# Block products for the output projection of tiles 5 and 6, wider transposes, and a new order of pieces, in an attention and cosine feed-forward kernel

## The chip, the cores and the metric

The kernel runs on one core of a Trainium2 chip. The core's engines work side by side, each through its own queue in order: TensorE (PE, matmuls; its weight loads are shown as PEld), VectorE (DVE), ScalarE (ACT), GpSimd (POOL), and SyncE (SP), which issues the transfers. The metric is the device time of one execution in microseconds; lower is better.

## The reference, cut to what matters

```python
# attention in chunks of 64 tokens: batch 8, heads 8, 576 tokens, head size 64
scores = scale * np.matmul(q_c, k_c.transpose(0, 1, 2, 4, 3))
scores = scores - np.max(scores, axis=-1, keepdims=True)
attn = np.exp(scores)
attn = attn / (np.sum(attn, axis=-1, keepdims=True) + 1e-09)
x = np.matmul(attn, v_c)            # laid out as 4608 tokens x 512
# feed-forward
h = x @ w_in                        # 512 -> 2048
g = h * np.cos(h)
out = g @ w_out                     # 2048 -> 512
```

## The kernel before

**Tiles and products.** The 4608 tokens are worked on in nine tiles of 512, t = 0 to 8. A product of float32 matrices is made of three fast matmuls: each operand is split into a high part (a cast, `g_hi`, L338 on DVE or L340 on ACT) and a low part (a subtraction, `g_lo`, L344), and high x high, high x low and low x high are added up in PSUM. Each output block is so 128 rows by 512 columns (128x512) or by 256 (128x256).

**Hidden product x @ w_in.** Tiles 0 and 1 are multiplied plainly, tile 2 with two-by-two blocks inside the tile (`two_pairs`). Tiles (3,4), (5,6) and (7,8) go as pairs, u = 1, 2, 3. For a pair the hidden columns are made in eight steps k, two column blocks at a time, with seven block products where eight would be plain: A11, S3, S2, A12, S1, A22, S4. Their sums are taken through PSUM: ACT copies one accumulator into the bank in which the next goes on (`copy_b`, `copy_c`, `copy_d`, L967), and DVE makes two additions (`add_c`, `add_b`, L970). The chain h -> g = h cos h is `whole` (ACT, L973), `turn` (DVE, L976), `sine` (ACT, L980) and `times` (DVE, L983). The bank that S4 fills is read by that chain, and the next step's `copy_b` can write its own bank only when a bank of this kind is free.

**Output projection g @ w_out.** Before, for u = 1 and 2 (`wide_pair`), it is plain: 128x512 matmuls into `acc`, 192 for each tile; the second tile's g is stored to DRAM (`gathered`) and read back (`second_tile`). For u = 3 (`block_pair` with `block_products`) it also goes by seven block products, P1 to P7, on 128x256 matmuls: DVE and POOL make sums of 128x256 blocks of g, the sums are stored to DRAM (`sums`) and loaded back with differences of w_out (`diffs`) for the later products.

**Attention.** Its pieces for later tiles are laid between the products: scores (64x64 matmuls), maximum, exponentials, sums, quotient, 32x32 transposes on DVE (`turned`, L636 and L640), and the weighted values. For (t, g) in `CHUNKED` the exponential of each 64-column chunk is its own ACT instruction, which also gives the sum; otherwise DVE subtracts the maximum, ACT takes the exponential of a wide piece, and DVE sums it. `wide_x` splits the attention's result of a pair of tiles into the fourteen parts that the seven hidden products need.

**Order.** The program is a list of pieces, `work`. `in_order(work, RANK, ELSEWHERE)` sorts it by the hand-kept table `RANK`, and `ELSEWHERE` lists pieces that run on their other engine (ACT for DVE, POOL for DVE). So each engine's queue follows that one order:

```python
place = sorted(range(len(work)), key=lambda i: (rank[i], i)) if rank else range(len(work))
return [(i, work[i][8][0] if i in elsewhere else work[i][0]) for i in place]
```

Of the kernel before, what the change touches and what calls it, by code (L numbers as in the profile page):

```python
# [44 lines left out]
CHUNKED = ((3, 1), (4, 1))  # L45
# [2453 lines left out]
```

## Time and profile before

| | |
|---|---|
| time, median of 3 runs | 776.09 us (774.72 to 777.68) |
| span of the profiled execution on the engines | 773.5 us |
| times of the three runs beside that span | 777.68, 774.72 and 776.09 us |
| PE busy | 762.5 us (99%), 6100 instructions |
| DVE busy | 644.4 us (83%), 1112 instructions |
| ACT busy | 444.8 us (58%), 818 instructions |
| POOL busy | 267.1 us (35%), 245 instructions |
| transfers | 177.22 MB, 66.2% of the 16 DMA engines' span on the main queue |

The profile is of one execution. The span is what the engines took from their first instruction to their last; the time of a run is the device's own and holds the span and some 2.6 us around it (776.09 less 773.5). Busy is the sum of an engine's instructions; a matmul's shown duration overlaps the next one's, so the rate of matmuls is read from a long unbroken row of them: its length over their number.

### The profile page before, as it was taken

The numbers are of one execution on the slowest core, as the hardware profiler recorded it, in microseconds if no ns is written. First come the engines' busy times: TensorE is split into PE (matmuls) and PEld (weight loads), VectorE is DVE, ScalarE is ACT, GpSimd is POOL, SyncE is SP. The second block draws the span as 40 slices with busy tenths as digits, with TensorE's granted clock in tenths as the row PEclk, the third lists the DMA queues.
The fourth block names the chain that finished last, engine by engine and source line by source line (L and its number), as shares of the span: only waits on it lengthen the run. The fifth ranks groups of instructions, "written<-read, shape, count | busy, mean of one in ns | idle before, by whom it ended". The sixth has DMA issues, their size and how long they took to land.

```text
span 773.5 us, 16085 instructions
## 1 busy us (share of the span) xinstructions
PE 762.5 (99%) x6100; PEld 676.3 (87%) x6100; DVE 644.4 (83%) x1112; ACT 444.8 (58%) x818; POOL 267.1 (35%) x245
## 2 busy tenths in 40 slices
PE   7999999999999999999999999999999999999997
PEld 6888888888999988888888888888888888989997
DVE  5998989989899889897898868785998577798874
ACT  5999876456874456554553435546554355557651
POOL 3422133776542444246222321200202315265231
PEclk9999999999999999999999999999999999999999
DMA  9995600579979753777974545587535567988983
GB/s 341 401 410 197 205 2 1 190 263 382 320 255 310 243 165 108 226 259 243 326 265 140 174 135 188 181 290 242 179 104 180 158 208 229 294 300 284 361 305 103
DMA packets 95757, 177.22 MB, mean 229 GB/s; under 512 B 9152, under 2 KB 39872, under 8 KB 95680
## 3 DMA queue, kind: packets, MB, share of 16 engines
q1 hardware_dynamic: 95104, 175.15, 66.2%
q8 instruction: 48, 0.79, 0.4%
q10 hardware_dynamic: 576, 1.05, 0.4%
q14 instruction: 29, 0.24, 0.1%
HBM read 127.93 MB, written 48.23 MB: 228 GB/s over the span
## 4 chain that ended last, share of the span: by engine, by line
PE 84%; DVE 8%; DMA 4%; ACT 2%; issue 1%; SPq 0%; DVEq 0%; ACTq 0%
PE acc L323 39%; PE h L323 33%; PE a L323 12%; DMA w_in<-sums 2%; DMA sums<-qt 1%; DMA combo<-w_in 1%; DVE w_in L970 1%; DMA kt<-in_kT_dram 1%; DVE z L595 0%; DVE w_in L344 0%; DVE pts L640 0%; DVE w_in L937 0%; DVE g L724 0%; DVE m L546 0%; DVE g L726 0%
## 5 line engine op out<-in xcount | busy, mean ns | idle before, releaser
L323 PE MATMUL acc<-w_out,g_hi 128*128 128x512 f32 (+1 forms) x976 | 278.1, 369 | 0.0
L323 PE MATMUL h<-x,w_in 128*128 128x512 f32 (+1 forms) x960 | 226.4, 364 | 0.1
L323 PEld LDWEIGHTS acc<-w_out,g_hi 128*128 128x128 f32 x976 | 178.5, 189 | 22.9
L323 PEld LDWEIGHTS h<-x,w_in 128*128 128x128 f32 x960 | 171.1, 189 | 22.7 <-ACT g_hi L340 0.4
L323 PE MATMUL acc<-w_out,g_lo 128*128 128x512 f32 (+1 forms) x488 | 179.2, 367 | 0.0
L344 POOL TENSOR_TENSOR g_lo<-g,g_hi 128x512 fp32r<-128x512 f32 x30 | 41.4, 1380 | 194.3 <-ACT g_hi L340 70.9
L323 PEld LDWEIGHTS acc<-w_out,g_lo 128*128 128x128 f32 x488 | 92.4, 189 | 11.8 <-DVE g_lo L344 0.2
L323 PE MATMUL h<-w_in,w_in 128*128 128x512 f32 (+1 forms) x384 | 98.3, 354 | 0.8 <-DVE w_in L970 0.7
L323 PEld LDWEIGHTS h<-w_in,w_in 128*128 128x128 f32 x384 | 65.6, 190 | 9.7 <-DVE w_in L970 2.0
L980 ACT ACTIVATE w_in<-w_in 128x512 f32<-128x512 f32 x64 | 39.3, 628 | 17.8 <-DVE w_in L976 17.7
L344 DVE TENSOR_TENSOR g_lo<-g,g_hi 128x512 fp32r<-128x512 f32 x59 | 44.1, 747 | 4.0 <-ACT g_hi L340 2.2
L340 ACT CAST g_hi<-g 128x512 fp32r<-128x512 f32 x48 | 29.7, 618 | 27.8 <-PE acc L323 14.5
L323 PE MATMUL a<-w_in,w_in 128*128 128x512 f32 (+1 forms) x204 | 42.5, 348 | 0.0
L323 PE MATMUL a<-x,w_in 128*128 128x512 f32 (+1 forms) x192 | 41.2, 353 | 0.0
L344 POOL TENSOR_TENSOR g_lo<-w_in,g_hi 128x512 fp32r<-128x512 f32 x12 | 18.9, 1577 | 64.3 <-ACT g_hi L340 42.6
L323 PEld LDWEIGHTS a<-w_in,w_in 128*128 128x128 f32 x204 | 34.5, 190 | 4.0
L323 PEld LDWEIGHTS a<-x,w_in 128*128 128x128 f32 x192 | 33.2, 190 | 4.1
L967 ACT COPY a<-h 128x512 f32<-128x512 f32 x28 | 16.0, 571 | 32.3 <-PE h L323 32.1
L723 ACT ACTIVATE g<-h 128x512 int32<-128x512 f32 x32 | 19.3, 602 | 26.1 <-PE h L323 26.0
L973 ACT ACTIVATE w_in<-h 128x512 int32<-128x512 f32 x32 | 19.1, 597 | 26.3 <-PE h L323 24.7
L976 DVE SCALAR_TENSOR_TENSOR w_in<-w_in,h 128x512 f32<-128x512 int32 x32 | 21.9, 685 | 12.6 <-ACT w_in L973 11.8
L344 DVE TENSOR_TENSOR g_lo<-w_in,g_hi 128x512 fp32r<-128x512 f32 x34 | 28.8, 855 | 3.8 <-ACT g_hi L340 3.2
(294 smaller groups left out, 1509.6 us busy)
## 6 DMA issues: line engine op xcount, KB each, us to landing
w_in<-combo SPq DMA_DIRECT2D x84, 512.0 KB, 4.8
combo<-w_in SPq DMA_DIRECT2D x56, 256.0 KB, 4.5
w_in<-combo SPq DMA_DIRECT2D x56, 256.0 KB, 5.3
qt<-in_qT_dram SPq DMA_DIRECT2D x36, 256.0 KB, 5.6
w_in<-in_w_in_dram SPq DMA_DIRECT2D x16, 512.0 KB, 9.7
kt<-in_kT_dram SPq DMA_DIRECT2D x32, 256.0 KB, 5.6
w_out<-in_w_out_dram SPq DMA_DIRECT2D x16, 512.0 KB, 9.9
gathered<-w_in SPq DMA_DIRECT2D x32, 256.0 KB, 3.7
```

What stands on the lines that cost most here:

```text
L323: kept(nc.tensor.matmul(*args, **kw))
L340: kept(nc.scalar.copy(out=out, in_=in_))
L344: kept(eng.tensor_tensor(out, a, b, op=op))
L723: lambda: kept(nc.scalar.activation(n, h, AF.Identity, bias=0.25, scale=0.5 / math.pi)),
L967: kept(nc.scalar.copy(out=out, in_=in_))
L970: kept(nc.vector.tensor_tensor(out, a, b, op=ALU.add))
L973: kept(nc.scalar.activation(g.bitcast(I32), h, AF.Identity, bias=0.25, scale=0.5 / math.pi))
L976: kept(nc.vector.scalar_tensor_tensor(g, g.bitcast(I32), -2.0 * math.pi, h, op0=ALU.mult, op1=ALU.add))
L980: kept(nc.scalar.activation(g, g, AF.Sin, bias=0.5 * math.pi))
```

## The change

Six things are changed.

- `BLOCKED` grows from the pair u = 3 to u = 2 and 3, so tiles 5 and 6 go through `block_pair` and `block_products` too.
- `CHUNKED` grows by (5,1), (6,1), (7,1), (8,1).
- `turned` takes a group of two head pairs at once: six transposes of twice the width take the place of twelve. Their room is one fixed `pair_room`.
- In each pair, S1 is issued ahead of A22 (in `block_pair` it was already), and `add_b` ahead of `add_c`, so S4 waits for the first addition and no longer for both.
- `times` may run on POOL where its input lies in SBUF.
- `RANK` and `ELSEWHERE` are new.

Counted over the whole program, before -> after: PE 128x512 matmuls 2736 -> 2352, 128x256 matmuls 1008 -> 1680, 64x64 groups of attention 29 -> 33 (in the first 30 us 8 -> 6). DVE transposes 168 of 256 columns -> 84 of 512; DVE casts of 512 columns -8, copies +4, reductions of 512 columns -8, subtractions of a maximum -8, additions of 128x256 48 -> 110, additions and products of 128x512 453 -> 431. ACT casts of 512 columns 163 -> 211, chunk exponentials of 64 columns on 128 partitions 40 -> 104, exponentials of 1024 columns 10 -> 2. POOL additions of 128x512 125 -> 193, of 128x256 114 -> 118. SP: 48 more stores of `sums` and 16 fewer of `gathered`, with the loads that go with them.

```diff
-CHUNKED = ((3, 1), (4, 1))
+CHUNKED = ((3, 1), (4, 1), (5, 1), (6, 1), (7, 1), (8, 1))
...
 RANK = (
-    35, 32, 39, 45, 48, 40, 16, 50, 63, 68, 66, 54, 72, 80, 85, 79, 75, 83, 89, 91, 92, 82, 97, 100, 104, 101, 88,
...
-    def turned(t, hp):
-
-        if t > 2 and hp >= 2:
-
-            pts = weights_of(t, 0)[:, hp % 2].rearrange("p c k -> p (c k)")
+    def turned(t, g):
+
+        if t > 2 and g:
+
+            pts = weights_of(t, 0).rearrange("p a c k -> p (a c k)")
         elif t == FAST + 2:
-            pts = half_room(U_ROOM, hp)
+            pts = w_in_room(U_ROOM, F32)[:, PAD : PAD + 2 * TOK]
         else:
-            pts = att.tile([P, TOK], F32, name="pts")
-        probs[t, hp] = pts
-        src = weights_of(t, hp // 2)[:, hp % 2].rearrange("p c (x k) -> p c x k", k=BL)
+            pts = pair_room.rearrange("p a n -> p (a n)")
+        for j in range(2):
+            probs[t, 2 * g + j] = pts[:, j * TOK : (j + 1) * TOK]
+        src = weights_of(t, g).rearrange("p a c (x k) -> p (a c) x k", k=BL)
...
-    def times(g, h):
-        kept(nc.vector.tensor_tensor(g, h, g, op=ALU.mult))
+    def times(g, h, by=DVE):
+        two_by(by, g, h, g, ALU.mult)
...
-    BLOCKED = range(UNITS - 1, UNITS)
+    BLOCKED = range(UNITS - 2, UNITS)
...
-        a22 = prod(A22, "c", cc)
-        s1 = prod(S1, "b", cc)
-        addc = piece(DVE, 0.69, add_c, a22, cd, *of("h2"))
-        addb = piece(DVE, 0.69, lambda: add(v["h3"], v["b"], v["ds"]), s1, cd, addc)
+        addb = piece(DVE, 0.69, add_b, s1, cd, *of("h2"))
+        addc = piece(DVE, 0.69, add_c, a22, cd, addb)
         s4 = prod(S4, "b", addb)
```

**The joint before tiles 7 and 8.** This is PE's queue where the weighted values of tile 8 are done and the hidden product of tiles 7 and 8 begins. Before, `acc` are the plain projections of tile 6 (102 matmuls of 128x512 in a row up to the first `h`), `x_0` and `x_1` are the high and low part for A11, and `x2` means two such in a row:

```order
L323 MATMUL acc_6925<-w_out_1327,g_hi 128x512 x2
L323 MATMUL acc_6925<-w_out_1327,g_lo 128x512
L323 MATMUL acc_6917<-w_out_1392,g_hi 128x512 x2
L323 MATMUL acc_6917<-w_out_1392,g_lo 128x512
L323 MATMUL h<-x_0_6943,w_in_6765 128x512
L323 MATMUL h<-x_1_7091,w_in_6765 128x512
L323 MATMUL h<-x_0_6943,w_in_6765 128x512 x2
```

The same place after the change, where the projections are block products of tiles 5 and 6:

```order
L336 MATMUL acc_7805<-w_in_7361,g_hi 128x256 x2
L336 MATMUL acc_7805<-w_in_7361,g_lo 128x256
L336 MATMUL acc_7805<-w_in_7361,g_hi 128x256 x2
L336 MATMUL acc_7805<-w_in_7361,g_lo 128x256
L336 MATMUL h<-x_0_7386,w_in_7166 128x512
L336 MATMUL h<-x_1_7398,w_in_7166 128x512
L336 MATMUL h<-x_0_7386,w_in_7166 128x512 x2
L336 MATMUL h<-x_1_7398,w_in_7166 128x512
L336 MATMUL h<-x_0_7386,w_in_7166 128x512
L336 MATMUL a_7873<-w_in_7783,w_in_7166 128x512
```

Ahead of A11 now stand 84 matmuls of 128x256 in a row in place of the 102 of 128x512, and behind A11 comes S3 (`a_7873`) at once.

**Between two steps of tiles 7 and 8.** PE's queue from the end of the first step to the A11 of the second. Before, projections (`acc`) stand between the last matmul of S4 (the first row) and A11 (`h<-x_0`); behind these rows come S3 and, after three more projections, S2:

```order
L323 MATMUL h<-w_in_7072,w_in_7104 128x512
L323 MATMUL acc_6939<-w_out_1554,g_hi 128x512 x2
L323 MATMUL acc_6939<-w_out_1554,g_lo 128x512
L323 MATMUL acc_6925<-w_out_1459,g_hi 128x512 x2
L323 MATMUL acc_6925<-w_out_1459,g_lo 128x512
L323 MATMUL acc_6917<-w_out_1554,g_hi 128x512 x2
L323 MATMUL acc_6917<-w_out_1554,g_lo 128x512
L323 MATMUL h<-x_0_6943,w_in_7104 128x512
L323 MATMUL h<-x_1_7091,w_in_7104 128x512
L323 MATMUL h<-x_0_6943,w_in_7104 128x512 x2
L323 MATMUL h<-x_1_7091,w_in_7104 128x512
L323 MATMUL h<-x_0_6943,w_in_7104 128x512
```

After, the rows begin with the last of S4 (`w_in_7886`); A11, S3 and S2 (`w_in_7764`) follow it:

```order
L336 MATMUL h<-w_in_7886,w_in_7525 128x512
L336 MATMUL h<-x_0_7386,w_in_7525 128x512
L336 MATMUL h<-x_1_7398,w_in_7525 128x512
L336 MATMUL h<-x_0_7386,w_in_7525 128x512 x2
L336 MATMUL h<-x_1_7398,w_in_7525 128x512
L336 MATMUL h<-x_0_7386,w_in_7525 128x512
L336 MATMUL a_7979<-w_in_7783,w_in_7925 128x512
L336 MATMUL a_7979<-w_in_7803,w_in_7925 128x512
L336 MATMUL a_7979<-w_in_7783,w_in_7925 128x512 x2
L336 MATMUL a_7979<-w_in_7803,w_in_7925 128x512
L336 MATMUL a_7979<-w_in_7783,w_in_7925 128x512
L336 MATMUL h<-w_in_7764,w_in_7925 128x512
```

The projections between are gone from this place; nothing but A11's six and S3's six matmuls stands between S4 and S2 here.

**Transposes and additions on DVE.** DVE's queue in a step of tiles 5 and 6, where an attention tile's weights are transposed (L640 and L636) between the two additions of the step (L970). Before, `a_6255` is the bank of `add_c`, `h` that of `add_b`:

```order
L640 STREAM_TRANSPOSE e_5749<-e_5786 32x8x32
L636 STREAM_TRANSPOSE e_5749<-e_5786 128x8x32
L976 SCALAR_TENSOR_TENSOR g<-g,h 128x512
L970 TENSOR_TENSOR w_in_6276<-a_6255,w_in_3870 128x512
L640 STREAM_TRANSPOSE e_5749<-e_5786 32x8x32
L970 TENSOR_TENSOR w_in_6276<-h,w_in_3870 128x512
L640 STREAM_TRANSPOSE e_5749<-e_5786 32x8x32 x3
L976 SCALAR_TENSOR_TENSOR w_in_6290<-w_in_6290,w_in_6276 128x512
L983 TENSOR_TENSOR g<-h,g 128x512
L976 SCALAR_TENSOR_TENSOR w_in_6290<-w_in_6290,h 128x512
L640 STREAM_TRANSPOSE e_5749<-e_5786 32x8x32
```

A like place after (the lines have moved: L640 to L664, L636 to L660, L970 to L994, L976 to L1000, L983 and L344 to L357):

```order
L619 TENSOR_SCALAR z<-z 128x16
L620 RECIPROCAL z<-z 128x16
L660 STREAM_TRANSPOSE pts<-w_in_6528 128x16x32
L664 STREAM_TRANSPOSE pts<-w_in_6528 32x16x32 x2
L1000 SCALAR_TENSOR_TENSOR w_in_6727<-w_in_6727,h 128x512
L994 TENSOR_TENSOR w_in_6743<-h,w_in_3823 128x512
L664 STREAM_TRANSPOSE pts<-w_in_6528 32x16x32
L357 TENSOR_TENSOR w_in_6727<-h,w_in_6727 128x512
L994 TENSOR_TENSOR w_in_6743<-a_6714,w_in_3823 128x512
```

The transposes are twice as wide, and the addition from `h` (`add_b`) stands ahead of the one from the `a` bank (`add_c`).

## Rows read from the trace of the kernel before

**Rows 1.** The page's span, and part 1: busy time by engine.

```profile
span 773.5 us, 16085 instructions
PE 762.5 (99%) x6100; PEld 676.3 (87%) x6100; DVE 644.4 (83%) x1112; ACT 444.8 (58%) x818; POOL 267.1 (35%) x245
```

**Rows 2.** PE's waits from 30 us on: releaser, us in total, times, longest.

```profile
PE h L323 <- DVE w_in L970: 0.7, 2, 0.4
...
PE h L323 <- DVE w_in L983: 0.3, 1, 0.3
```

**Rows 3.** Windows: stretch, its us; each engine's busy us, clock, DMA share, GB/s.

```profile
0.00:30.00 30.00, 25.09 (x446) 21.59 (x447) 21.15 (x47) 21.57 (x52) 10.77 (x14) 1.00 0.97 361
...
540.00:600.00 60.00, 60.00 (x508) 52.53 (x499) 53.52 (x96) 30.24 (x51) 12.23 (x10) 1.00 0.46 155
585.00:612.00 27.00, 27.00 (x126) 23.54 (x125) 22.97 (x31) 9.80 (x18) 9.50 (x7) 1.00 0.63 205
```

**Rows 4.** The chain that ended last, three pieces: start us, us, engine, tile, line.

```profile
412.60 13.60 PE acc L323 x63
...
584.75 22.24 PE acc L323 x102
...
734.47 11.46 PE acc L323 x102
```

**Rows 5.** PE's timeline around an attention group: start us, us, operation.

```profile
461.71 0.38 PE L323 MATMUL acc<-w_out,g_lo 128*128 128x512 f32 x1
462.02 0.27 PE L323 MATMUL h<-kt,qt 64*64 64x64 f32 x1
...
463.90 0.22 PE L323 MATMUL a<-kt,qt 64*64 64x64 f32 x1
464.05 0.70 PE L323 MATMUL acc<-w_out,g_hi 128*128 128x512 f32 x2
464.58 0.38 PE L323 MATMUL acc<-w_out,g_lo 128*128 128x512 f32 x1
```

**Rows 6.** Groups by shape: busy us, mean ns of one, idle before.

```profile
L344 DVE TENSOR_TENSOR g_lo<-g,g_hi 128x512 fp32r<-128x512 f32 x59 | 44.1, 747 | 4.0 <-ACT g_hi L340 2.2 <-DMA w_in<-sums 0.3
L344 POOL TENSOR_TENSOR g_lo<-g,g_hi 128x512 fp32r<-128x512 f32 x30 | 41.4, 1380 | 194.3 <-ACT g_hi L340 70.9 <-DVE g_hi L338 67.1 <-PE h L323 30.7
...
L340 ACT CAST g_hi<-g 128x512 fp32r<-128x512 f32 x48 | 29.7, 618 | 27.8 <-PE acc L323 14.5 <-DVE g L983 4.7 <-issue 4.4
L344 DVE TENSOR_TENSOR g_lo<-w_in,g_hi 128x512 fp32r<-128x512 f32 x34 | 28.8, 855 | 3.8 <-ACT g_hi L340 3.2
L983 DVE TENSOR_TENSOR w_in<-w_in,w_in 128x512 f32<-128x512 f32 x32 | 25.2, 786 | 3.1 <-ACT w_in L980 3.0
...
L983 DVE TENSOR_TENSOR w_in<-h,w_in 128x512 f32<-128x512 f32 x32 | 21.9, 686 | 4.3 <-ACT w_in L980 3.5
...
L640 DVE STREAM_TRANSPOSE pts<-e 32x256 f32<-32x256 f32 x40 | 17.0, 432 | 0.9
...
L558 ACT ACTIVATE w_in<-a,m 128x64 f32<-128x64 f32 x16 | 4.9, 348 | 0.5 <-issue 0.5
...
L344 DVE TENSOR_TENSOR w_in<-w_in 128x256 f32<-128x256 f32 x9 | 4.4, 513 | 0.1
```

**Rows 7.** Timeline of all engines after an S4, in tiles 7 and 8.

```profile
660.78 1.46 PE L323 MATMUL h<-w_in,w_in 128*128 128x512 f32 x6
...
662.27 0.60 ACT L973 ACTIVATE w_in<-h 128x512 int32<-128x512 f32 x1 [1.35 <-PE h L323]
...
665.07 0.57 ACT L967 COPY h<-h 128x512 f32<-128x512 f32 x1 [0.81 <-DVE w_in L983]
```

**Rows 8.** DVE's timeline at the parts of tiles 7 and 8.

```profile
592.74 0.69 DVE L344 TENSOR_TENSOR vt<-e,pts 128x512 f32<-128x512 f32 x1
593.34 1.77 DVE L344 TENSOR_TENSOR w_in<-pts,x 128x512 fp32r<-128x512 f32 x1
```

**Rows 9.** The page's part 6, transfers: count, size each, median us from issue to landing.

```profile
w_in<-combo SPq DMA_DIRECT2D x84, 512.0 KB, 4.8
```

More of the change, by code (lines that the diff above doesn't have):

```diff
@@ L428, in attention_then_cos_ffn, with pts_room @@
     probs = {}
+    pair_room = att.tile([P, 2, TOK], F32, name="pts", bufs=1)
+    asked_pts = [-1]
+    def pts_room():
+        asked_pts[0] += 1
+        return pair_room[:, asked_pts[0] % 2]
     asked_x = [-1, -1]
@@ L1237, in attend_third, with go @@
         for g in range(2):
-            pts = []
-            for hp in (2 * g, 2 * g + 1):
-                key = ("t", t, hp)
-                def go(key=key, hp=hp):
-                    made[key] = turned(t, hp)
-                    made[key][0]()
-                pts.append(piece(DVE, 0.44, go, q[hp], w, *partial_out))
-                for i in range(1, 6):
-                    pts.append(piece(DVE, 0.44, rest_of(key, i), pts[-1]))
+            key = ("t", t, g)
+            def go(key=key, g=g):
+                made[key] = turned(t, g)
+                made[key][0]()
+            pts = [piece(DVE, 0.7, go, q[2 * g], q[2 * g + 1], w, *partial_out)]
+            for i in range(1, 6):
+                pts.append(piece(DVE, 0.7, rest_of(key, i), pts[-1]))
             key = ("x", t, g)
@@ L1507, in chain @@
         a = piece(ACT, 0.21 + 0.42 * s, lambda: sine(g()), a, table=AF.Sin)
-        return w, piece(DVE, 0.14 + 0.55 * s, lambda: times(g(), h()), a, port=port)
+        return w, piece(
+            DVE, 0.14 + 0.55 * s, lambda by=DVE: times(g(), h(), by), a, port=port, other=(POOL, 1.05, False) if port else None,
+        )
     def h_bank():
@@ L1559, in copy_d, with rooms_of_h, add_b @@
             copy(v["ds"], v["d"])
+        def rooms_of_h():
+            if "h2" not in v:
+                room = w_in_room(H_ROOM, F32)[:, PAD : PAD + 2 * TOK]
+                v["h2"], v["h3"] = room[:, :TOK], room[:, TOK:]
         def add_c():
-            room = w_in_room(H_ROOM, F32)[:, PAD : PAD + 2 * TOK]
-            v["h2"], v["h3"] = room[:, :TOK], room[:, TOK:]
+            rooms_of_h()
             add(v["h2"], v["c"], v["ds"])
+        def add_b():
+            rooms_of_h()
+            add(v["h3"], v["b"], v["ds"])
         pieces = {}
@@ L1573, in two_pairs @@
         prod(A12, "a", cb)
+        prod(S1, "b", cc)
         prod(A22, "c", cc)
-        prod(S1, "b", cc)
-        addc = piece(DVE, 0.69, add_c, done[A22], cd, *of("h2"))
-        addb = piece(DVE, 0.69, lambda: add(v["h3"], v["b"], v["ds"]), done[S1], cd, addc)
+        addb = piece(DVE, 0.69, add_b, done[S1], cd, *of("h2"))
+        addc = piece(DVE, 0.69, add_c, done[A22], cd, addb)
         prod(S4, "b", addb)
@@ L1637, in copy_d, with rooms_of_h, add_b @@
             copy(v["ds"], v["d"])
+        def rooms_of_h():
+            if "h2" not in v:
+                room = w_in_room(H_ROOM, F32)[:, PAD : PAD + 2 * TOK]
+                v["h2"], v["h3"] = room[:, :TOK], room[:, TOK:]
         def add_c():
-            room = w_in_room(H_ROOM, F32)[:, PAD : PAD + 2 * TOK]
-            v["h2"], v["h3"] = room[:, :TOK], room[:, TOK:]
+            rooms_of_h()
             add(v["h2"], v["c"], v["ds"])
+        def add_b():
+            rooms_of_h()
+            add(v["h3"], v["b"], v["ds"])
         prod(A11, "a", *of(ha), begin=h_bank)
@@ L1812, in copy_d, with rooms_of_h @@
             copy(v["ds"], v["d"])
+        def rooms_of_h():
+            if "h2" not in v:
+                room = w_in_room(H_ROOM, F32)[:, PAD : PAD + 2 * TOK]
+                v["h2"], v["h3"] = room[:, :TOK], room[:, TOK:]
         def add_c():
-            room = w_in_room(H_ROOM, F32)[:, PAD : PAD + 2 * TOK]
-            v["h2"], v["h3"] = room[:, :TOK], room[:, TOK:]
+            rooms_of_h()
             add(v["h2"], v["c"], v["ds"])
         def add_b():
+            rooms_of_h()
             add(v["h3"], v["b"], v["ds"])
@@ L1833, in block_pair @@
         a22 = prod(A22, "c", cc)
-        addc = piece(DVE, 0.69, add_c, a22, cd, *of("h2"))
-        addb = piece(DVE, 0.69, add_b, s1, cd, addc)
+        addb = piece(DVE, 0.69, add_b, s1, cd, *of("h2"))
+        addc = piece(DVE, 0.69, add_c, a22, cd, addb)
         s4 = prod(S4, "b", addb)
@@ L2055, in new_rows @@
             elif i:
-                rows[i, name] = att.tile([P, TOK], F32, name={"A": "pts", "B": "pts", "C": "vt", "D": "vt"}[name])
+                rows[i, name] = room_named({"A": "pts", "B": "pts", "C": "vt", "D": "vt"}[name])
             elif name in "AB":
@@ L2240, in scores_now, with begin @@
             z = piece(DVE, 0.45, lambda g=g: inverse(t, 2 * g, 2 * g + 2), *totals, port=True)
-            for hp in (2 * g, 2 * g + 1):
-                q = piece(
-                    DVE, 0.69, lambda by, hp=hp: quotient(t, hp, by), z, port=True, other=(POOL, 1.3, False)
-                )
-                key = (t, hp)
-                def begin(key=key):
-                    made[key] = turned(*key)
-                    made[key][0]()
-                if hp >= 2:
-                    free = [ends[hp - 2]]
-                elif t == FAST + 2:
-                    free = [stored_sums["six"], ends.get(0)]
-                else:
-                    free = weighed.get(t - 1, ())
-                a = piece(DVE, 0.44, begin, q, *free)
-                for i in range(1, 6):
-                    a = piece(DVE, 0.44, lambda i=i, key=key: made[key][i](), a)
-                ends[hp] = a
+            q = [
+                piece(DVE, 0.69, lambda by, hp=hp: quotient(t, hp, by), z, port=True, other=(POOL, 1.3, False))
+                for hp in (2 * g, 2 * g + 1)
+            ]
+            key = (t, "turned", g)
+            def begin(key=key, g=g):
+                made[key] = turned(t, g)
+                made[key][0]()
+            if g:
+                free = [ends[0]]
+            elif t == FAST + 2:
+                free = [stored_sums["six"]]
+            else:
+                free = weighed.get(t - 1, ())
+            a = piece(DVE, 0.7, begin, *q, *free)
+            for i in range(1, 6):
+                a = piece(DVE, 0.7, lambda i=i, key=key: made[key][i](), a)
+            ends[g] = a
         turned_all[t] = ends
@@ L2273, in weighted_now @@
             both.append(pe(
-                1.06, go, *of(names[g][0]), *of(names[g][1]), *(turned_all[t][2 * g + j] for j in range(2)),
+                1.06, go, *of(names[g][0]), *of(names[g][1]), turned_all[t][g],
                 values_here.get((t, g)),
@@ L2312, in go @@
                 def go(by, j=j, name=name, a=a, b=b, cc=cc, value=value):
-                    found[j, cc] = att.tile([P, TOK], F32, name=name)
+                    found[j, cc] = room_named(name)
                     second = value(b) if b in (S1, S2) else x(*b, cc)
```

22 lines of the change are left out of this document (13 added, 9 removed), and 380 rows, old and new, of tables (ELSEWHERE, RANK).

## The prediction

> **What bounds the kernel now.** I read the page's busy times first: PE 762.5 of 773.5 us, DVE 644.4, ACT 444.8, POOL 267.1 [rows 1]. PE is full, so the next question is where it is not. Its list of waits from 30 us on is short; the two lines that matter here are a matmul behind DVE's additions (L970), 0.7 us in two waits, and one behind `times` (L983), 0.3 us [rows 2]. The other gap is the start: in the first 30 us PE is busy for 25.09 us [rows 3]. The granted clock is 1.00 in every stretch read, which is the 2.4 GHz level, so there is no clock to win. PE's rate comes from unbroken rows in the chain that ended last: 63 matmuls of 128x512 in 13.60 us, 0.2159 us each, and 102 of 128x256 in 11.46 us, 0.1124 us each [rows 4]. The kernel is therefore bound by the number of columns that PE streams; what a change is worth is the columns removed, less the new waits of PE.
>
> **The change part by part.**
>
> *Matmuls.* 384 of 128x512 go (two tiles of 192), 672 of 128x256 come. 384 x 0.2159 = 82.9 us; 672 x 0.1124 = 75.5 us: -7.4 us. Eight products become seven, but a half-size matmul costs 52% of a whole one, so of the eighth (10.4 us) 3 us are lost. The Trainium skill ("TensorE: Matmul & The Clock Gate", section "Wait — 56ns, not 53.3ns?") gives the warm spacing as N / 2.4 GHz + about 2.5 ns: 215.8 and 109.2 ns. The row for 512 columns agrees, the one for 256 is 3 ns slower; by that rule the saving would be an estimated 9.5 us. I keep the rows, since these are the same operation in the same program.
>
> *Attention groups.* PE's switch into a group of 64x64 matmuls begins 0.31 us after the last wide matmul instead of 0.216 (461.71 to 462.02), and on leaving it 0.15 us pass from the last small matmul to the first wide one, and the next two wide ones take 0.53 instead of 0.43 (464.05 to 464.58) [rows 5]: about 0.33 us a group. There are 4 more: +1.3 us.
>
> *S1 before A22, `add_b` before `add_c`.* S4 then waits for one addition with six matmuls (1.3 us) ahead of it, against 0.69 us for the addition [rows 6]. The 0.7 us of waits on L970 go: -0.7 us.
>
> *Cover behind S4.* The next step's `copy_b` needs the bank that S4's chain reads. In the trace of before S4's six matmuls begin at 660.78, so their slot ends at 662.08; ACT's L973 starts at 662.27, three more links follow, and `copy_b`, released by DVE's L983, runs from 665.07 to 665.64 [rows 7]. S2 can start 3.56 us after S4. Before, A11, S3 and 12 projections (24 x 0.2159 = 5.2 us) lie between them in the first steps of tiles 7 and 8. After, the order shows only A11 and S3 there: 12 x 0.2159 = 2.6 us, so PE waits 1.0 us. At one place of tiles 5 and 6 six projections of 256 columns stand with them (2.6 + 0.7 = 3.3 us): 0.3 us. Elsewhere the cover is longer than 3.6 us. +1.3 us; bounds 0.7 (the chain found idle engines) and 4 (each link queued behind one other instruction of 0.69 us).
>
> *The joint of tiles 7 and 8.* Between tile 8's weighted values and A11 stand 84 matmuls of 256 columns, 9.4 us, for 102 of 512, 22.24 us [rows 4]. Behind it DVE and ACT make fourteen parts and eight differences: 14 low parts and 8 differences at 0.69 [rows 8], and some casts, 15 to 20 us of DVE; over this work of before DVE was busy for 22.97 of 27.0 us [rows 3]. Only A11's two parts and S3's first must be ready at once; from there PE has 12 projections and 72 hidden matmuls, 9.4 + 2.6 + 1.3 + 15.6 = 28.9 us in all against 15 to 23 us. It fits on average, but the parts come in the order in which they are consumed, so a late one stops PE. I take +0.5 us; bounds 0 and 4.
>
> *DVE.* Removed: 168 transposes at 0.432 become 84 of twice the width. No row shows that width: if it were free, -36 us; if it were proportional, 0. Another 256 columns of an addition cost 0.747 - 0.513 = 0.234 us [rows 6], so I take 0.67 each, -17 us. Eight casts, eight reductions and eight subtractions go, at the 0.69 of an addition or a little less, -15 us; 62 additions of 256 columns come, at 0.513, +32 us; 22 of 512 go, at 0.75, -16 us; copies and small ones +4. Sum -12 us: 632 us. Nothing of that is on PE's path by itself; it keeps DVE at 82%.
>
> *ACT and POOL.* ACT: 48 casts at 0.618, 64 chunk exponentials at 4.9 / 16 = 0.31 [rows 6], less eight exponentials of 1024 columns at twice the 0.62 of 512: about +40 us, 485 of 766, at 63% hidden behind PE. POOL: 68 additions at 1.38 us and 4 small ones, +97 us, 364 us (48%); it has the room, but see the rival below.
>
> *Transfers.* Sums of 10.5 MB are stored and loaded back and 4 MB of differences loaded; 16 stores of g of 256 KB go, and their loads (8.4 MB): about 17 MB more, at 0.46 to 0.63 of the DMA engines' time where it falls [rows 3]. A load of 512 KB lands 4.8 us after its issue [rows 9], and the pieces are asked for many matmuls ahead, which hides it; I cost it at nothing, bounds 0 and one landing, 4.8 us.
>
> *The start.* Two attention groups leave the first 30 us, where PE stands for 4.9 us [rows 3]. I cost it at nothing, bounds -2 and +1.
>
> Sum: -7.4 + 1.3 - 0.7 + 1.3 + 0.5 = -5.0 us on a span of 773.5, 768.5. The runs' median lies 2.6 us above the span (776.09), and I keep that: **771.1 us**.
>
> **The rivals.**
>
> *Clean.* The order hides all of S4's chain and of the joint, the start gains a microsecond: -7.4 + 1.3 - 0.7 - 1 = -7.8, 768.3 us. For it: before, these two waits come to 1.0 us in all [rows 2], with DVE as full. Against it: the 2.6 us of cover, which the rows put 1 us short.
>
> *DVE held up by POOL.* DVE's instructions with two operands in SBUF are longer than the one with an operand in PSUM (0.686): 0.747, 0.786 and 0.855 on average [rows 6], and one takes 1.77 us beside its neighbour of 0.69, so 1.08 us is the most that a row shows lost at once [rows 8]. The Trainium skill ("SBUF — State Buffer", section "SBUF: two separate sides") says that such a DVE instruction and a GpSimd one that reads SBUF exclude each other for the whole instruction. By that rule the 1.77 is one full block, and the trace agrees that such blocks happen. The means of the rows say less: 125 instructions of the three groups are 12.6 us over 0.686 (59 x 0.061 + 34 x 0.169 + 32 x 0.100), for 267 us of POOL; were all such DVE instructions (about 300) held alike, 0.12 us for each POOL instruction, 9 us for 72. The tight stretch is 540 to 600 us, where DVE is busy for 53.5 of 60 us [rows 3] and in which the softmax of tile 7 now meets the block sums of tiles 5 and 6. It would hold some 25 of the 72. PE begins to wait when each costs DVE over 0.3 us (25 x 0.3 = 7.5 us). At 0.4 us PE waits 4 us: 775, no change.
>
> *Slower, by the same mechanism at its full price.* At 0.75 us each, 25 instructions take 18.8 us out of 6.5 us of room, PE waits 12 us: 783 us. It decides from about 0.65 us per instruction. For it speaks the single 1.77, against it the means.
>
> *Loads late.* SP issues in order; sums of tiles 5 and 6 queued behind stores that wait for DVE would stop a row of projections for one landing, 4.8 us [rows 9]: 776, no change.
>
> **How the numbers follow.** Forecast 0.45, clean 0.25, held up 0.14, loads late 0.05, slower 0.11. A change of 0.5%, 3.9 us, is about what this measurement can tell from none: under 772.2 counts as faster, over 780.0 as slower. Of the forecast's range (769.5 to 773.5) three quarters lie under 772.2: faster 0.45 x 0.75 + 0.25 = 0.59; same 0.11 + 0.14 + 0.05 = 0.30; slower 0.11. The range for 8 in 10 reaches from the clean case with a gain at the start of 2 us (767) to the held-up case with both bounds of the cover (778).
>
> **What would show it.** Right: rows of 128x256 at 0.112 us in the projections of tiles 5 and 6; PE's busy time lower by 6 to 7 us; no waits of PE on L994 (the additions); one wait of about 1 us of a PE matmul on ACT's copy or L357 after the first step of tiles 7 and 8; DVE at about 635 us and transposes near 0.67 us. Wrong: transposes at 0.86 us (DVE 17 us more); DVE's two-operand groups well over 0.86 us on average, with PE waiting for DVE's parts or additions at 540 to 600 us; PE waiting for DMA into `w_in` or `combo`.

## The result, and the profile after

The changed kernel takes 785.11 us (median of four runs, 784.26 to 786.51) against 775.59 for the kernel before beside it: ratio 1.0121, 95% interval 1.0103 to 1.0139. It is 9.5 us slower (9.4 by the ratio); 771.1 us, 5 us faster, was forecast.

Part 1 of the page of the changed kernel, to be laid beside [rows 1]:

```profile
span 783.0 us, 17090 instructions
PE 762.7 (97%) x6388; PEld 681.7 (87%) x6388; DVE 647.8 (83%) x1056; ACT 486.7 (62%) x991; POOL 358.8 (46%) x317
```

PE's share falls from 99 to 97%, though its columns are fewer. That they are fewer shows in the chain that ended last (start us, us, engine, tile, line): 120 matmuls of 128x256 in 13.40 us are 0.1117 us each, close to the 0.1124 of [rows 4].

```profile
590.35 13.40 PE acc L336 x120
...
567.29 6.98 PE a L336 x46
```

The second of these rows is not at that rate: 0.152 us each. So part of the loss lies in waits and part in the clock. PE's waits of the changed kernel from 30 us on (releaser, us in total, times, longest), for [rows 2]:

```profile
PE h L336 <- DVE g L750: 2.6, 2, 1.7
PE acc L336 <- POOL g_lo L357: 1.8, 1, 1.8
PE a L336 <- ACT w_in L578: 1.7, 2, 1.0
PE a L336 <- ACT g_hi L353: 1.3, 1, 1.3
PE h L336 <- ACT h L991: 1.3, 3, 0.5
PE acc L336 <- DVE g_lo L357: 0.8, 1, 0.8
PE h L336 <- DVE w_in L994: 0.8, 2, 0.4
PE a L336 <- DVE g_lo L357: 0.8, 1, 0.8
```

1.6 us in five waits have become some eleven us in fifteen (two of 0.2 us are left out above), for three engines, none longer than 1.8 us. The windows (columns as in [rows 3]) show where the largest lie:

```profile
0.00:20.00 20.00, 15.02 (x246) 13.59 (x248) 10.65 (x26) 10.60 (x32) 5.82 (x11) 0.94 0.92 343
20.00:40.00 20.00, 19.04 (x240) 16.24 (x237) 18.53 (x36) 17.73 (x31) 11.14 (x9) 0.97 1.03 402
160.00:180.00 20.00, 18.34 (x202) 15.37 (x201) 19.15 (x29) 10.97 (x24) 16.52 (x17) 1.00 0.48 164
540.00:560.00 20.00, 17.86 (x88) 15.16 (x87) 18.92 (x31) 13.95 (x30) 13.75 (x15) 1.00 0.84 254
560.00:580.00 20.00, 17.89 (x138) 17.35 (x137) 16.83 (x30) 13.92 (x25) 4.21 (x4) 0.91 1.00 328
720.00:740.00 20.00, 18.15 (x163) 17.96 (x162) 19.40 (x34) 12.69 (x23) 8.72 (x4) 1.00 1.02 343
```

An account by such windows: columns -7.4, four attention groups +1.3 (both as forecast, the second not measured apart), PE's idle time between 20 and 760 us about +10 (11.7 against 1.9 before), the granted clock +3.6 (0.06 and 0.03 of the first two windows and 0.09 of 560 to 580, by 20 us each). That makes 7.5 of the 9.5 us between the spans. The other 2 us fit an estimate: in an unbroken row a matmul of 512 columns is shown for 0.38 us and the next begins after 0.22, so each of the ten waits more costs about 0.16 us beyond the idle time shown. The clock's share is less sure than the windows make it: one of the four executions had a mean clock of 0.998, and still took 784.26 us.

The longest wait but one, 1.66 us at 173 us, is this piece of the chain that ended last (start us, us, engine, tile, line):

```profile
167.57 3.97 DVE w_in L357 x4
...
172.83 0.70 DVE g L750
...
173.58 2.86 PE h L336 x12
```

The first row is four low parts of 128x256. They take 1.34, 1.50, 0.41 and 0.95 us, where the shortest of their kind takes 0.41, and the chain of g for which PE waits stands behind them. POOL runs two-operand instructions beside them nearly all the time. Before, all 32 low parts of this kind were on POOL; the new order has nine of them on DVE. So one wait can be of place and of load at once.

### The profile page after: what moved, and what is told of

Its sections match the earlier page's. It is cut to its first block, busy times and chain, and to the rows that moved or that the text cites. A ratio compares the mean times of both kernels' runs of the same rounds, so it can differ in the third digit from the quotient of the medians.

```text
span 783.0 us, 17090 instructions
## 1 busy us (share of the span) xinstructions
PE 762.7 (97%) x6388; PEld 681.7 (87%) x6388; DVE 647.8 (83%) x1056; ACT 486.7 (62%) x991; POOL 358.8 (46%) x317
## 4 chain that ended last, share of the span: by engine, by line
PE 71%; DVE 11%; ACT 6%; issue 4%; DMA 4%; POOL 2%; SPq 1%; DVEq 0%; ACTq 0%; POOLq 0%
PE acc L336 32%; PE h L336 26%; PE a L336 12%; DVE w_in L357 2%; DMA kt<-in_kT_dram 1%; POOL w_in L357 1%; DMA w_in<-diffs 1%; ACT w_in L578 1%; DVE g_lo L357 1%; DVE w_in L1000 1%; DMA w_in<-in_w_in_dram 1%; POOL g_lo L357 1%; DVE pts L664 1%; ACT w_in L1004 1%; DVE e L357 1%
## 5 line engine op out<-in xcount | busy, mean ns | idle before, releaser
L336 PE MATMUL acc<-w_out,g_hi 128*128 128x512 f32 (+1 forms) x848 | 225.4, 353 | 0.0
L336 PEld LDWEIGHTS acc<-w_out,g_hi 128*128 128x128 f32 x848 | 150.5, 190 | 17.3
L336 PE MATMUL acc<-w_out,g_lo 128*128 128x512 f32 (+1 forms) x424 | 148.5, 350 | 0.8 <-DVE g_lo L357 0.8
L336 PEld LDWEIGHTS acc<-w_out,g_lo 128*128 128x128 f32 x424 | 80.5, 190 | 9.7 <-DVE g_lo L357 1.6
L357 POOL TENSOR_TENSOR w_in<-w_in,w_in 128x512 f32<-128x512 f32 (+2 forms) x37 | 46.7, 1269 | 81.7 <-ACT w_in L1004 41.9
L357 POOL TENSOR_TENSOR g_lo<-g,g_hi 128x512 fp32r<-128x512 f32 x30 | 44.2, 1475 | 72.9 <-DVE g_hi L351 33.5
L336 PEld LDWEIGHTS h<-w_in,w_in 128*128 128x128 f32 x384 | 65.7, 190 | 11.7 <-ACT h L991 2.7
L357 POOL TENSOR_TENSOR g_lo<-w_in,g_hi 128x512 fp32r<-128x512 f32 x23 | 31.5, 1375 | 47.1 <-ACT g_hi L353 37.6
L353 ACT CAST g_hi<-w_in 128x512 fp32r<-128x512 f32 x52 | 32.2, 624 | 25.1 <-PE a L336 9.0
L357 DVE TENSOR_TENSOR g_lo<-w_in,g_hi 128x512 fp32r<-128x512 f32 x47 | 39.1, 839 | 9.0 <-ACT g_hi L353 7.9
L997 ACT ACTIVATE w_in<-w_in 128x512 int32<-128x512 f32 x40 | 25.0, 625 | 14.0 <-DVE w_in L994 13.1
L357 DVE TENSOR_TENSOR g_lo<-g,g_hi 128x512 fp32r<-128x512 f32 x35 | 28.1, 802 | 6.6 <-ACT g_hi L353 6.2
```

Source lines behind the costliest of these rows:

```text
L336: kept(nc.tensor.matmul(*args, **kw))
L353: kept(nc.scalar.copy(out=out, in_=in_))
L357: kept(eng.tensor_tensor(out, a, b, op=op))
L997: kept(nc.scalar.activation(g.bitcast(I32), h, AF.Identity, bias=0.25, scale=0.5 / math.pi))
```

## The experiments

The theory at first was one of places: about a dozen waits, each with its own instruction that stands behind others in its engine's queue. Its rival was load: DVE and POOL hold each other up, and there is no room left for what the change adds. The comparisons below are with the kernel before, run beside each.

**Single pieces, and the products of the chains.** One low part of g (`g_lo`) went from POOL to DVE by one number less in `ELSEWHERE`; in the other run 36 `times` went from POOL back to DVE.

> The changed kernel with one instruction moved from POOL to DVE: the low part of a block of g for which PE waits 2.0 us at 738 us. In the trace it takes 4.9 us on POOL, where its like take 1.3, while DVE runs five instructions with two operands in SBUF one after the other. Theory 1 with the exclusion of the two engines as its mechanism: the wait goes, 1.5 to 2 us less, 783 to 783.6 us. If that instruction was late for another reason (its operand, a transfer): the wait stays at the same place, 785 us.

> The changed kernel with all 36 multiplications g = h cos h that run on POOL put back on DVE at the same place in the order: 36 x 0.69 = 25 us more on DVE, 49 us less on POOL. If the exclusion of the two engines is the larger cost: DVE's long instructions get fewer, and the time falls by 2 to 5 us, to 780 to 783 us. If the place in DVE's queue is the larger cost (DVE is at 83% and busier around the waits): PE waits longer, 786 to 793 us.

Measured: 781.79 us, 1.0090 (1.0066 to 1.0114), and 790.92 us, 1.0210 (1.0175 to 1.0246). The piece was worth 2.4 us by the two ratios (their intervals leave 0 to 5); its wait, 1.8 us, is gone. Its two timelines in the changed kernel, POOL and then DVE (start us, us, engine, line), say why:

```profile
733.49 4.89 POOL L357 TENSOR_TENSOR g_lo<-g,g_hi 128x512 fp32r<-128x512 f32 x1 [7.01 <-ACT g_hi L353]
```

```profile
733.15 0.69 DVE L357 TENSOR_TENSOR x<-w_in,x 128x512 fp32r<-128x512 f32 x1
733.76 0.42 DVE L357 TENSOR_TENSOR kt<-w_in,kt 128x256 f32<-128x256 f32 x1
734.09 0.69 DVE L357 TENSOR_TENSOR w_in<-w_in 128x512 fp32r<-128x512 f32 x1
...
737.17 1.76 DVE L357 TENSOR_TENSOR w_in<-w_in,w_in 128x512 fp32r<-128x512 f32 x1
738.85 0.68 DVE L357 TENSOR_TENSOR w_in<-w_in 128x512 fp32r<-128x512 f32 x1
```

POOL's subtraction takes 4.89 us where others take 1.38 [rows 6]: a row of DVE instructions of 0.42 and 0.69 us runs through at full speed beside it (733.76 to 737.17), and then one of DVE takes 1.76. The Trainium skill ("SBUF — State Buffer", section "SBUF: two separate sides") has the two engines exclude each other for a whole instruction; this row agrees, and shows that the one that waits can be POOL, and for several instructions. Taking all 36 products off POOL is worse by 6.9 us: DVE is then busy for 664.5 us, 16.7 us more.

**Whole new orders.** Six kernels had `RANK` and `ELSEWHERE` written anew by a program that searched for an order by fixed durations. Two re-ordered all pieces and chose their engines anew (for the changed kernel and for the kernel before), two re-ordered only the queues of DVE, ACT and POOL (without and with PE's), one had everything but the block products of tiles 5 and 6, one the old `CHUNKED`.

> The changed kernel's pieces, all of them, in another order and with another choice of engine for the pieces that may run on DVE or POOL: a search that gives each engine some slack and lets a two-operand DVE instruction and a POOL instruction exclude each other. Theory 1 (the loss is in the order: pieces on DVE, ACT and POOL are queued so tightly that they come late): the waits of PE after 40 us fall from some 12 us to under 3 us, and the 7.4 us of matmuls saved show: 766 to 772 us. Theory 2 (the loss is the added work on DVE, ACT, POOL and the queues of transfers, which no order hides): the waits move elsewhere, 780 us or more. Theory 3 (the matmuls of 128x256 are slower in these places): PE's busy time stays and no wait goes, 783 us or more.

> The kernel before with its pieces in an order from the same search: what the order alone gives. Theory 1: the kernel before waits for only 1 us after 30 us, so it gains at most that and 2 to 3 us at the start: 771 to 776 us; the re-planned changed kernel is then 4 to 7 us faster than this one. Theory 2: 771 to 776 us too, but the re-planned changed kernel is slower than this one.

> The changed kernel with only the order of the pieces on DVE, ACT and POOL changed, by a search that starts from its order and asks for slack (it must also do with durations 3% longer and 50 ns more from engine to engine); PE's queue, the queue of transfers and every piece's engine are as in the changed kernel. The first two re-planned kernels were slower because PE then waited for transfers and for a DVE that had taken over POOL's work; here neither is moved. Theory 1 (the loss is in the order within the queues of DVE, ACT and POOL): the waits after 40 us halve, 774 to 779 us. Theory 2 (the added work itself): the waits go elsewhere, 783 us or more.

> Everything of the change but the block products of tiles 5 and 6 (BLOCKED holds only the last pair of tiles, as before): transposes two head pairs at a time, exponentials by chunk, the swapped additions. Its order is that of the kernel before, with the new pieces where the old ones stood, put through the same search as the run beside it. Theory 1: these parts cost little themselves and give back none of the 7.4 us, so 773 to 779 us, a few us above the same search's kernel with the block products or level with it. Theory 2 (the block products' own work is what makes PE wait): it is faster than the kernel with block products by 3 us or more, at 770 to 774 us.

> The changed kernel with the exponentials by chunk only where the kernel before has them (four of the six new places undone), the order from the same search. ACT then has some 19 us less of short exponentials, DVE some 9 us more. If the chunk exponentials in ACT's queue are what delays the copies on which PE waits (ACT behind its own exponentials at 541 us), it is 2 to 3 us faster than the kernel of the same search with them; if they are neutral, level with it within 1.5 us.

> As the first run of this call, with the order of PE's pieces free too, so that projections can stand between S4 and the next step's S2 again. If the cover behind S4 is a large part of the loss (the copies at 475, 515, 553, 640 and 669 us cost 2.9 us in all in the changed kernel): 2 to 4 us faster than the first run of this call, 771 to 776 us. If not: level with it.

Measured, in this order: 812.20 (1.0490), 801.96 (1.0348), 825.13 (1.0656), 813.89 (1.0510), 821.74 (1.0615) and 823.70 us (1.0637). All are slower than what they were made from, so they tell little of the parts that they leave out: without the block products it is 11 us better than the like order with them, with the old chunks 3.4 us better, and an order alone moves the time by more than either. That is what they do show. The third has the same instructions as the changed kernel, in another order:

```profile
PE 775.6 (94%) x6388; PEld 682.8 (83%) x6388; DVE 690.5 (84%) x1056; ACT 485.8 (59%) x993; POOL 362.0 (44%) x317
```

DVE is busy for 690.5 instead of 647.8 us: 43 us in which its instructions were longer, and only the order of the queues differs. The increase is spread over many groups, nearly all of instructions with two operands. A search with fixed durations can't see this.

**Seventeen small moves** of an order, each meant to take one wait away, on top of the one piece.

> The changed kernel with one piece of tiles 5 and 6 (a low part of g) on DVE, as in the run with one piece moved, and 17 pieces moved by a few places in the queues of DVE, ACT and POOL: the copies ahead of the second chain's matmuls before the casts and output copies that stood ahead of them, parts ahead of sums that nobody waits for. No instruction is added or taken away. Theory of places (the 10 to 13 us lost are a dozen waits of 0.5 to 2 us, each from an instruction that stands behind others in its engine's queue): each wait can be taken away where it stands; 781.8 less about 5 to 7 us, 775 to 777. Rival, load (DVE and POOL carry too much work together, and hold each other up wherever the order puts them): a wait taken away comes back at the next place, 780 to 783. Rival, collisions (each small change of order shifts which DVE instruction meets which POOL instruction, for better or worse by several us): 783 or more, with DVE's busy time up by over 5 us.

Measured: 786.67 us, 1.0147 (1.0122 to 1.0173), worse than without the moves. The theory of places falls in its simple form: the wait for `times` (L750) grew from 2.5 to 3.8 us while others shrank. The time is in the range of the rival, collisions; DVE's busy time rose by 4.5 us over the kernel with one piece moved, a little under the 5 us that this rival asked for.

**Load added to the kernel before.** Four kernels add 72 instructions on a spare tile, three in each of 24 steps, which nobody reads:

```diff
+    spare = const.tile([P, 448], F32, name="spare")
+    nc.vector.memset(spare, 0.0)
+    def idle_work():
+        tc.keep_in_program_order(nc.gpsimd.tensor_tensor(spare, spare, spare, op=ALU.add))
...
         def add_c():
+            idle_work()
```

`copy_b` and `copy_c` begin with `idle_work()` in the same way. The others have `nc.vector` there, `nc.gpsimd.memset(spare, 0.0)`, and `nc.scalar.copy`. A fifth adds the POOL additions to the changed kernel.

> The kernel before, with 72 additions of 448 columns on a spare tile added on POOL (three in each of 24 steps, where the changed kernel has 72 more POOL instructions of about 1.3 us); nothing reads them, so they can cost only through POOL's own queue and through what they hold up on DVE. Theory of load: DVE's busy time rises by 10 us or more, and the time by 5 us or more, to 780 or above. Theory of places: POOL is at 35% and DVE's order stands; 774 to 777, DVE's busy time up by 5 to 15 us, hidden.

> The kernel before, with 72 additions of 448 columns on a spare tile added on DVE at the same places (about 0.6 us each, 43 us of DVE's time). Theory of load: DVE goes from 644 to about 690 us, 89% of the span, and PE waits for it: 780 or above. Theory of places: the time moves only where a wait already stood, 775 to 778. Whichever, it gives a price of DVE time: the loss divided by 43 us; the changed kernel has only 3.4 us more on DVE than the kernel before.

> The changed kernel with the same 72 additions added on POOL (POOL then at about 440 us, 57%). Theory of load: the slack is used up already, so it loses more than the kernel before does with the same additions: 792 or above. Theory of places: the loss is like that of the kernel before with the same additions, within 3 us.

> The kernel before with 72 memsets of 448 columns on a spare tile added on POOL, at the places where the run with POOL additions has additions: they take POOL's queue, write SBUF and read nothing. If the additions cost their 8.7 us by holding up DVE while they read: 774 to 777 here, and DVE's busy time near 644 instead of 666. If they cost it in POOL's queue: the loss is in proportion to the time that a memset takes there, 778 or above where it takes 0.5 us or more.

> The kernel before with 72 copies of 448 columns on a spare tile added on ACT at the same places (about 0.55 us each, 40 us, as much as the change adds to ACT). If ACT's load delays the copies behind the second chain and the parts: 777 to 780. If ACT at 58% hides it: 774 to 776.

| added | to | time, us | ratio (95%) |
|---|---|---|---|
| POOL additions | before | 783.49 | 1.0112 (1.0092 to 1.0132) |
| DVE additions | before | 786.47 | 1.0150 (1.0128 to 1.0172) |
| POOL memsets | before | 775.11 | 1.0002 (0.9989 to 1.0016) |
| ACT copies | before | 774.82 | 0.9996 (0.9982 to 1.0011) |
| POOL additions | changed | 808.52 | 1.0434 (1.0414 to 1.0454) |

Part 1 of the pages of the first four, in this order:

```profile
PE 764.6 (98%) x6100; PEld 674.5 (86%) x6100; DVE 666.2 (85%) x1113; ACT 444.5 (57%) x818; POOL 342.9 (44%) x317
```

```profile
PE 764.6 (97%) x6100; PEld 675.0 (86%) x6100; DVE 693.4 (88%) x1185; ACT 445.2 (57%) x818; POOL 273.9 (35%) x245
```

```profile
PE 762.0 (99%) x6100; PEld 675.2 (87%) x6100; DVE 650.8 (84%) x1113; ACT 445.3 (58%) x818; POOL 296.9 (38%) x317
```

```profile
PE 763.1 (98%) x6100; PEld 675.2 (87%) x6100; DVE 644.8 (83%) x1113; ACT 476.2 (61%) x890; POOL 267.8 (35%) x245
```

72 POOL additions, which nobody waits for, make DVE busy for 21.8 us more with one instruction more (666.2 against 644.4 in [rows 1]), 0.30 us each, and cost 8.7 us by the ratio. The largest group of PE's waits is on the additions L976 (L970 in the kernel before), 3.4 us in three:

```profile
PE h L329 <- DVE w_in L976: 3.4, 3, 1.7
```

49 us more on DVE cost 11.6 us, 0.24 us for each us. These are prices at the places tried: one of the three additions of a step stands right ahead of `add_c`, behind which S4 waits. No other places were tried. 31 us more on ACT cost nothing. The memsets, 0.48 us each and so half as long on POOL, give DVE 6.4 us and the time nothing; whether they would at the additions' length was not tried. In the changed kernel the same additions cost some 24 us instead of 8.7, with 28.7 us more on DVE. Here the rival, load, has the better of it.

**Load taken from the changed kernel.** The sums of tiles 5 and 6 are made on 16 of 256 columns (the output of these tiles is left out in part); in the second run the 36 products on POOL on 16 of 512 columns too.

```diff
-                two_by(by, at["s", o], at[a], at[b], op)
+                n = HALF if ends else 16
+                two_by(by, at["s", o][:, :n], at[a][:, :n], at[b][:, :n], op)
...
-        two_by(by, g, h, g, ALU.mult)
+        n = 16 if by == POOL else TOK
+        two_by(by, g[:, :n], h[:, :n], g[:, :n], ALU.mult)
```

> The changed kernel with the 64 sums and differences of tiles 5 and 6 (36 on DVE, 28 on POOL) made on 16 of their 256 columns, and a spare tile stored in their place, so that the sums of these tiles, and the output of tiles 5 and 6, are left out in part; every instruction, wait and transfer stands where it stood. DVE has about 15 us less, POOL about 20 us less. Theory of load, at the prices of the kernel before (11.2 us for 72 DVE additions that took 49 us, 8.7 us for 72 of POOL): 15 x 0.23 + 28 x 0.12 = 6.8 us, 776 to 780. Rival, order (the waits stand where the order puts them, whatever the load): within 2 us of the changed kernel's 785.

> As the run with thin sums, and the 36 products of the chains that stand on POOL made on 16 of 512 columns too (a part of g is left out). POOL has about 65 us less than in the changed kernel, near what it had before. Theory of load: a further 36 x 0.12 = 4.3 us, and about a microsecond for each place where the matmuls waited for such a product, 769 to 775: the forecast of 771 would then have been right for the columns, and wrong for what the sums cost. Rival, order: 780 or above.

Measured: 783.84 us, 1.0105 (1.0055 to 1.0155), and 780.19 us, 1.0066 (1.0047 to 1.0086). The first lies by its median in the rival's range, order, but is uncertain: its executions spread from 776.5 us of span, at a mean clock of 1.000, to 785.9, at 0.990. The second is at the edge of the rival's range and far from load's 769 to 775: it gives back 4.3 us by the ratios for 55 us of POOL and 21 us of DVE, where the prices above had promised 11. So load is not all, and its price in the kernel before does not carry over. The longest waits that stay, in the second run:

```profile
PE h L338 <- DVE g L752: 2.6, 2, 1.7
PE h L338 <- ACT h L993: 1.3, 3, 0.6
PE a L338 <- ACT w_in L580: 1.3, 2, 0.7
PE a L338 <- ACT g_hi L355: 1.1, 1, 1.1
```

The first three stand where they stood in the changed kernel, the 1.66 us at 173 us (174 here) among them. The last is for the high part of a sum that was stored and loaded back.

**The clock at the start.** The kernel before shows a mean clock of 0.999 or 1.000 in each of the fourteen executions beside these two runs, the changed one 0.993 to 0.998 in its own. The new order moves a group of score matmuls of the second tile on PE, from between two groups of transposes (12.8 us) to 18.8 us. One kernel moves it back in the kernel with the one piece on DVE, the other moves it away in the kernel before, with its three successors on DVE and ACT:

```diff
 L634 MATMUL a<-ident,e 128x128 x4
+L336 MATMUL a<-kt,qt 64x64 x32
 L336 MATMUL acc<-pts,vt 64x64 x32
...
-L336 MATMUL a<-kt,qt 64x64 x32
```

> The changed kernel with the low part of g on DVE as in the run with one piece moved (781.8 us, 779 to 783 by its executions), and one group of score matmuls of the second tile (16 of 64x64) moved back on PE from behind the fourth group of weighted values to behind the first transposes, where the kernel before has it. Nothing else moves. Theory of the clock (a PE that idles near 13 us is given the lower level from 16 to 21 us): the granted clock stays at 1.00 in the first 40 us, the executions show a mean clock of 0.998 or more, and the time is 778 to 780. Rival (the clock falls for another reason, or the group only shifts the work by its own 1.1 us): clock and time as in the run with one piece, 781 to 783.

> The kernel before with the same group of score matmuls moved to behind the second group of weighted values, as the changed kernel has it, and its three successors on DVE and ACT moved behind their neighbours as far as that asks. No work is added. Theory of the clock: the clock falls to 0.5 to 0.7 for some 4 us between 14 and 22 us in most executions, the mean clock is 0.993 to 0.998, and the time grows by 2 to 4 us, to 777 to 779. Rival (nothing but the place of 1.1 us of matmuls): 774 to 776 at a clock of 1.000.

Windows of 2 us, first of the changed kernel, then of the kernel before with the group moved, then of the one with the group moved back (the last figure but two is the clock):

```profile
12.00:14.00 2.00, 1.31 (x11) 0.85 (x8) 1.97 (x6) 1.71 (x3) 0.99 (x2) 1.00 1.05 403
14.00:16.00 2.00, 0.88 (x34) 0.84 (x35) 1.56 (x5) 1.73 (x4) 1.45 (x2) 1.00 1.03 401
16.00:18.00 2.00, 1.12 (x12) 0.65 (x12) 1.78 (x6) 1.20 (x4) 0.80 (x2) 0.92 1.06 412
18.00:20.00 2.00, 2.00 (x55) 2.00 (x56) 1.61 (x5) 1.48 (x4) 1.58 (x2) 0.50 1.01 399
20.00:22.00 2.00, 2.00 (x52) 1.71 (x48) 1.19 (x3) 0.76 (x3) 0.59 (x1) 0.73 1.06 399
```

```profile
12.00:14.00 2.00, 0.43 (x4) 0.42 (x4) 1.90 (x8) 1.96 (x4) 1.04 (x1) 1.00 1.05 396
14.00:16.00 2.00, 1.50 (x38) 1.20 (x36) 1.85 (x4) 2.00 (x5) 1.53 (x2) 0.65 1.04 404
16.00:18.00 2.00, 2.00 (x47) 1.67 (x47) 1.54 (x3) 1.76 (x6) 2.00 (x2) 0.50 1.05 408
18.00:20.00 2.00, 2.00 (x29) 1.82 (x26) 1.09 (x3) 0.87 (x3) 0.51 (x1) 0.50 1.01 395
20.00:22.00 2.00, 2.00 (x37) 1.47 (x35) 1.54 (x5) 0.56 (x3) 0.52 (x1) 0.64 1.04 393
```

```profile
12.00:14.00 2.00, 1.52 (x58) 1.41 (x61) 1.72 (x5) 1.76 (x4) 1.11 (x2) 1.00 1.05 404
18.00:20.00 2.00, 1.75 (x58) 1.45 (x61) 2.00 (x5) 1.99 (x6) 1.39 (x2) 1.00 1.02 404
```

In the changed kernel PE had waited for 1.66 and 0.88 us, in the kernel with the group moved for 1.92 us, when the clock fell to the 1.2 GHz level. It stayed there for 3.4 and 6.8 us, by these windows. In the kernel before, whose longest wait there is 0.91 us, it stayed at 1.00. It is not a matter of the order alone: the profiled execution of the kernel with the one piece, in the order of the changed kernel, waited for 1.20 and 0.88 us and kept 1.00.

In the kernel before, the move alone brings the fall about (mean clock 0.994 to 0.997 in seven of eight executions) and costs 2.1 us: 776.58, 1.0027 (1.0016 to 1.0037), the lower end of the growth that was expected. How much of that is the clock is not shown: the eighth execution, at 1.000, took 775.85 us. Moved back, the clock is 0.998 to 1.000, but the time is 780.93 us, 1.0097 (1.0074 to 1.0119), the same as with the one piece alone. There the expectation failed. PE is busy for 33.55 of the first 40 us, against 34.60 in the profiled execution of the kernel with the one piece, both at a clock of 1.00: in its old place the group brought other waits of about 1 us.

No kernel here beats the one before; the best that does all of the work of the changed one is 0.9% slower.

## Why the prediction was wrong

- *Matmuls*, -7.4: right, by the rate in the chain's row. The sign that went with it, PE's busy time lower by 6 to 7 us, did not show (762.7 against 762.5), since the low clock lengthens matmuls; where the clock stayed at 1.00, in the kernel with the group moved back, it is 758.9, 3.6 lower.
- *Cover behind S4*, +1.3: right as a sum, by luck. There are 1.3 us in three waits on ACT's copy (L991), but 0.9 of them in tiles 5 and 6 (0.55 at 475 us, 0.37 at 553), where 0.3 was forecast, and 0.35 in tiles 7 and 8 (640 us), where it was 1.0.
- *S1 and `add_b`*, -0.7: wrong; PE still waits for L994, 0.8 us in two (515 and 669 us), against 0.7 for L970.
- *ACT and POOL*: 486.7 and 358.8 us against 485 and 364, right as totals. That ACT's work is hidden was right for load (the run with 31 us more), wrong for place: chunk exponentials (L578) stop a product twice, for 1.7 us, since it goes into the bank that they read.
- *DVE*: 632 us forecast, 647.8 measured. The transposes are near the forecast, 0.70 instead of 0.67 us, 3 us in all; the rest fits instructions held up. What DVE's instructions take over the median of their own operation and shape sums up to 61 us, against 49 before. Two groups stand at 0.80 and 0.84 us (0.75 and 0.86 in [rows 6]) where the undisturbed one takes 0.69:

```profile
L357 DVE TENSOR_TENSOR g_lo<-w_in,g_hi 128x512 fp32r<-128x512 f32 x47 | 39.1, 839 | 9.0 <-ACT g_hi L353 7.9 <-PE a L336 0.2
L357 DVE TENSOR_TENSOR g_lo<-g,g_hi 128x512 fp32r<-128x512 f32 x35 | 28.1, 802 | 6.6 <-ACT g_hi L353 6.2
L664 DVE STREAM_TRANSPOSE pts<-e 32x512 f32<-32x512 f32 x20 | 14.0, 702 | 0.5
```

- **The step that failed** is the sentence behind it, "Nothing of that is on PE's path by itself", and with it the price of nothing for 97 us more on POOL. DVE had no room to spare: at the places tried in the kernel before, PE lost 0.24 us for each us more of DVE's work and 0.12 us for each POOL addition that nobody waits for. In the changed kernel DVE is held up by some 12 us more, and with most of the added load taken away 4.3 of the 9.4 us come back, while the held-up time falls to 48 us, no more than before. So the load is worth about 4 us. The 8.7 us that 72 additions cost before are not its price here.
- What the sum had *no term* for are single waits that the new order and the new block products make: 1.66 us at 173 us, where DVE makes low parts that POOL made before, and those at the joints below.
- The forecast's *rival* "slower, by the same mechanism at its full price" gave 783 us, at a chance of 0.11. The runs bear out its mechanism in part; its size and its place were wrong, so that the number is near is luck. It wanted 0.65 us for each instruction within 540 to 600 us; measured are 0.30 us each in the kernel before, and the waits come all along from 160 to 740 us. In 540 to 580 PE idles for 4.25 us and loses 1.8 by the clock, half of the 12 us that it put there. Of the 4.25 us, 0.98 are for a chunk exponential, 0.37 for the copy, 1.56 for low parts on DVE (559 and 567 us), and 1.34 for the high part of a sum loaded back (566 us). *Loads late* has a share in the last that no run separates.
- *The joint of tiles 7 and 8*, +0.5 with bounds 0 and 4: it cost next to nothing. A11 begins at 625.9 us, and PE has no wait from 568 to 632 us; the first two behind are 0.22 us (ACT's copy, 633) and 0.25 us (DVE, 637). The forecast had no term for the other joint of a pair, where its last hidden step meets the first block products. For tiles 5 and 6 three of the waits above stand there, 2.9 us (559 to 567), with the 1.8 us by the clock behind them; for tiles 7 and 8 it is the 1.8 us on POOL's low part at 738 us.
- *The start*, 0 with bounds -2 and +1: it lost 1 us of waiting and 1.8 by the clock. Which group left the start was read from the order; that the clock can fall behind PE's idle time there was not asked, as the rows of before show 1.00 throughout.

How the rest divides is not settled. With most of the added load taken away 5.1 us over the kernel before remain, by the ratio; moving places, or single pieces to another engine, made no kernel faster by more than 2.4 us. That the remaining waits come of the order alone is argued from where they stand, not shown.

## What to carry to other kernels

A share of 83% on an engine was no room here: price the slack of each engine in the kernel at hand, by a few dozen idle instructions on it at the places where the work will land, before forecasting that added work is hidden. Such a price holds for its kernel and its places: taken over to the changed kernel, it promised 11 us and gave 4. Count POOL's additions as DVE's time too (0.30 us each here). Where work is moved out of a stretch in which TensorE already idles, look at the granted clock behind it, and cost each joint that the change makes, not only the one that exists already.

## What was not expected of the hardware

- The same instructions in another order of the queues kept DVE busy for 690.5 instead of 647.8 us.
- A subtraction on POOL took 4.89 instead of 1.38 us while DVE ran a row of instructions on SBUF without a pause.
- After waits of 1.66 and 0.88 us the granted clock was 0.50 for 3.4 us at 18 us, though PE was busy again. After waits of 1.34 and 0.77 us at 566 us 128x256 matmuls went at 0.21 us each for some 3 us:

```profile
566.03 0.49 PE L336 MATMUL a<-w_in,g_hi 128*128 128x256 f32 x2 [1.34 <-ACT g_hi L353]
567.29 0.58 PE L336 MATMUL a<-w_in,g_lo 128*128 128x256 f32 x1 [0.77 <-DVE g_lo L357]
567.66 0.64 PE L336 MATMUL a<-w_in,g_hi 128*128 128x256 f32 x2
568.09 0.42 PE L336 MATMUL a<-w_in,g_lo 128*128 128x256 f32 x1
568.30 0.63 PE L336 MATMUL a<-w_in,g_hi 128*128 128x256 f32 x2
```
